# Storing half of the output earlier: the residual sum of the first 256 channels moved next to their inverse transform, and a new order for the whole program

## The chip, the cores and the metric

The kernel runs on one core of a Trainium2 chip. The metric is the device time of one execution in microseconds (us), lower being better. A core has one TensorE (PE, matmuls), VectorE (DVE), ScalarE (ACT), GpSimd (POOL, almost unused here) and SyncE (SP). In this kernel SP alone issues the transfers (DMAs) between DRAM and the on-chip memory (SBUF).

## What is computed

The input `u` has 2048 positions (tokens) of 512 channels. The result is the input plus a long convolution along the positions, scaled by a gate that an MLP computes:

```python
x = A_u
xn = _layernorm(x, axis=-1)
s = _A_ref(xn, A_A_re, A_A_im, A_B_re, A_B_im, A_C_re, A_C_im, A_log_dt, A_Dskip)
g = _silu(_B_ref(xn, B_w1, B_w2, B_w3, B_w4))
return x + s * g
```

`_A_ref` builds, for each channel, a kernel of 2048 taps from 128 complex exponentials, and convolves it with `xn` by a transform of length 4096 (`Kf = rfft(K)`, `Uf = rfft(u)`, `irfft(Uf * Kf)`), plus `u * Dskip`. `_B_ref` mixes tokens (`gelu(layernorm @ w1)`, a shift of each quarter of the channels by one or two positions, `@ w2`) and then runs an MLP of width 1376 (`gelu(layernorm(x1) @ w3) @ w4`), both with a residual.

## The kernel before

The tokens lie on the 128 partitions, 16 on each, so the result `X` is a tile of 128 x 16 x 512 float32. In DRAM the same data is addressed as `xv` (input) and `ov` (output) in four pieces of 32 partitions, `by_r` (L578), so every load of the input and every store of the result is four DMAs. `X` is worked on in eight groups `g` of two of the sixteen rows.

The stages are: loads; token mixing (layer norm, `w1`, `w2`); tables of exponentials for the convolution kernels (DVE and ACT); the first transform stage of the kernels (`kstage1`: results go to DRAM as `scr_Kfa` and `scr_Kfb`); the products of the spectra (`products`: loads `cst`, `uin`, `kin`, stores `scr_Zda`, `scr_Zdb`); the MLP (`w3` into the `pb` banks, gelu, `w4` into the `pa` banks); the gate, a silu on `X`; the inverse transform (`inverse(hf, g)`, L895: it loads a tile `zin` of 128 x 4 x 256, runs 16 small matmuls into a pair of `pc` or `pd` banks, and multiplies the pair into `X` on DVE); and `finish(g)`, L911. The convolution is done for two halves of the channels, `hf` 0 and 1, with 256 channels each (`DH`): letter a or b at the end of a scratch name is the half.

`finish(g)` loads the input again (the tiles `xr`, one for two groups, four DMAs of 32 x 2048), adds it to both halves of the group, 128 x 1024 elements in one DVE instruction, and stores the group with four DMAs of 32 x 1024, 128 KB each. It can only follow the inverse of both halves.

The order of the instructions is not written out by hand. Every step (`due`, L572) gives a due time to the instructions that follow it: a base from a few constants plus one entry of the table `SHIFT`. A list scheduler (`Plan.order`) places each instruction on its engine by the due times, dependences and modelled costs. It sets the order on PE, ACT, DVE and SP, and which of ACT and DVE makes some copies. Instructions of one engine then run in that order: one that waits holds all behind it, and that includes SP's DMAs. All instructions are issued from one line of a helper, L310 in the kernel before and L313 in the changed one, so the profile tells them apart by tiles.

Tiles that are reused are in rings: the loads of `zin` for the first half go round five buffers, those of the second half have eight.

Of the kernel before, what the change touches and what calls it, by code (L numbers as in the profile page):

```python
# [10 lines left out]
F32 = mybir.dt.float32  # L11
# [8 lines left out]
P = 128  # L20
L = 2048
D = 512
# [61 lines left out]
class Op:  # L84
# [10 lines left out]
SAME = {"PE": 0.0, "ACT": 0.13, "DVE": 0.1, "SP": 0.0}  # L95
TABLE_LOAD = 1.41
DMA_RATE = 300e3
LAND, PAD = 2.45, 0.16
BASE, FINE, END = 16512, 19840, 229368

KGC, QUAD = 3.25, 0.95
WARM = 40

SHIFT = (
# [21 lines left out]
)  # L126
Q0, QC = -778.0, 0.05
SWITCH = 2279.26
PREFERP, AVOIDP = 2674.41, 272.51
PREFER, AVOID = 3332.92, 790.65  # L130
PV, T0, TC = 257.0, 396.7, 309.52
LX, LC, LP, LW, LV = -4000.0, 0.11, -3964.6, -2693.7, -3696.7
M0, MC, WC = 807.9, 710.86, 0.25
H0, HC, SC = -3530.1, 638.4, 0.22
KA, PA, PAC, FA = -1045.1, -3015.7, 0.25, 592.1
KB, PB, PBC, FB = -157.1, -136.4, 0.08, 323.0
FC = 0.29


def mlp_due(g, jp):  # L140
# [3 lines left out]
class Plan:  # L144
# [105 lines left out]
    def order(self):  # L250
# [17 lines left out]
        while len(out) < len(ops):  # L268
# [4 lines left out]
            for o in pools[e]:  # L273
                if o.ready <= t + 0.02:
                    v = o.vt
                    if e == "ACT" and o.table and o.table != table:
                        v += SWITCH
                    if len(o.alts) > 1:
# [141 lines left out]
def kernel(  # L420
# [9 lines left out]
    V, A, T, Q = [Engine(plan, e) for e in ("DVE", "ACT", "PE", "SP")]  # L430
    E = Either(plan)

    xv = u[0].rearrange("(t r s) d -> r t s d", r=4, s=S)
    ov = out[0].rearrange("(t r s) d -> r t s d", r=4, s=S)
# [5 lines left out]
    DH = D // 2  # L440
# [7 lines left out]
    def area(nbytes):  # L448
        o = place[0]
        place[0] = o + nbytes  # L450
        assert place[0] <= END
        return o

    def at(offset, shape, dt, name):
        return nc.alloc_sbuf_tensor_at(name, shape, dt, offset=offset)[:]
# [37 lines left out]
    X = at(area(4 * S * D), [P, S, D], F32, "X")  # L493
    K2, K4 = 2048, 4096
# [8 lines left out]
    early = area(11 * K2)  # L503
# [25 lines left out]
    o = late + 8 * K4  # L529
# [10 lines left out]
        ),  # L540
    ]

    zinr = [Ring(early, K4, 5), Ring(o, K4, 8)]
    xrs = [late + 2 * K4 * k for k in range(3)] + [o + 10 * K4]
    assert o + 12 * K4 <= END

# [12 lines left out]
    def pp_pair():  # L559
        turn["pp"] += 1  # L560
        return bank[2 + turn["pp"] % 2]
# [9 lines left out]
    def due(t=None):  # L571
        plan.stage += 1  # L572
        t = plan.base = plan.base if t is None else t
        plan.vt = t + (SHIFT[plan.stage] if plan.stage < len(SHIFT) else 0)


    def by_r(sb, dr, to_dram=False):

        for r in range(4):
            a, d = sb[32 * r : 32 * r + 32], dr[r]  # L580
            Q.dma_start(d, a) if to_dram else Q.dma_start(a, d)
# [307 lines left out]
    def gate(g):  # L889
        due(FA + FC * g)  # L890
        X2 = X[:, 2 * g : 2 * g + 2]
        A.activation(X2, X2, AF.Silu)

    def inverse(hf, g):
        due((FA, FB)[hf] + FC * g)  # L895
        ch = slice(hf * DH, hf * DH + DH)
        zin = zinr[hf]([P, 4, DH], F32, "zin")
        Q.dma_start(zin, Zd[hf][:, 2 * g : 2 * g + 2, :, :, :].rearrange("r s e g d -> (s e g) r d"))
        py = [t[:, :DH] for t in pp_pair()]
        with plan.together(cost=0.55):  # L900
            for r in range(4):
                for a in range(2):
                    h = slice(64 * a, 64 * a + 64)
                    T.matmul(py[a][32 * r : 32 * r + 32], is2[h], zin[h, r], start=True, stop=True)
        for a in range(2):
            Xh = X[:, 2 * g + a, ch]
            V.tensor_mul(Xh, Xh, py[a])

    xr = []

    def finish(g):  # L911
        due(FB + FC * g)
        if g % 2 == 0:
            xr.append(at(xrs.pop(), [P, 4, D], F32, "xr"))
            by_r(xr[-1], xv[:, :, 2 * g : 2 * g + 4])
        X2 = X[:, 2 * g : 2 * g + 2]
        V.tensor_add(X2, X2, xr[-1][:, 2 * (g % 2) : 2 * (g % 2) + 2])
        by_r(X2, ov[:, :, 2 * g : 2 * g + 2], to_dram=True)


    def pow2_scale(cols, dst_s, dst_inv, target):
# [296 lines left out]
    for hf in range(2):  # L1218
        for g in range(8):
            inverse(hf, g)  # L1220
    for g in range(8):
        finish(g)
    with nc.allow_non_contiguous_dma(reason="parameters by state"), tc.manual_schedule():
# [26 lines left out]
```

## Time and profile before

| | us |
|---|---|
| median of 3 runs (lowest to highest) | 673.48 (673.35 to 673.55) |
| the profiled execution | 674.49 |
| its span in the profile | 672.7 |
| busy in the span: PE, weight loads (PEld) | 625.8 (93%), 414.4 |
| busy in the span: DVE, ACT | 540.7 (80%), 480.6 (71%) |

The page of the profile gives busy times of engines, and the chain of work that ended last, followed back from the last instruction. The table of windows gives the busy time of each engine in a stretch of the span, with the granted TensorE clock as a share of full speed and the share of the DMA engines in use. The timeline gives instructions in order of time. The sequencer of SP, which issues the DMAs, is called SPq; the duration of a DMA row is the time it held that sequencer, not the transfer. Times in the rows count from the start of the span.

### The profile page before, as it was taken

The page shows a single profiled execution, that of the slowest core. Times are in us where ns is not written, and L with a number is a line of the kernel's source. Part 1 is how long each engine was busy: PE and PEld are TensorE (multiplying, and loading weights), DVE is VectorE, ACT ScalarE, POOL GpSimd, SP SyncE. Part 2 cuts the span into 40 slices and gives each one's busy share as a digit, 9 for nine tenths or more (in the row PEclk, how much of TensorE's full clock was granted, in tenths as well). Part 3 has the DMA queues.
Part 4 walks back from the last instruction along what each step waited for, and adds up shares of the span by engine and source line. Part 5 has one row for each costly group of instructions (what it writes and reads, how often), then busy time and mean ns, then how long its engine had stood idle before and what let it go on. Part 6 is the DMA issues. An engine that isn't in the chain of part 4 may idle for free.

```text
span 672.7 us, 13855 instructions
## 1 busy us (share of the span) xinstructions
PE 625.8 (93%) x5526; PEld 414.4 (62%) x5526; DVE 540.7 (80%) x798; ACT 480.6 (71%) x1050; POOL 0.7 (0%) x6
## 2 busy tenths in 40 slices
PE   7489979899995999898999999999999999999984
PEld 7457858466464686665687576676675756556531
DVE  5898899999999999988999999998434154454557
ACT  3889899969938999987999999994246353223420
POOL 0000000000000000000000000000000000000000
PEclk9899999899998899998999999999999999999995
DMA  8955252422121111385343324328599568854997
GB/s 230 235 166 187 82 183 88 147 77 79 32 79 55 56 45 37 72 226 167 79 131 91 105 65 129 98 77 206 151 271 267 141 142 219 203 159 137 249 304 218
DMA packets 100751, 95.60 MB, mean 142 GB/s; under 512 B 48656, under 2 KB 81424, under 8 KB 99792
## 3 DMA queue, kind: packets, MB, share of 16 engines
q1 hardware_dynamic: 100688, 94.73, 50.3%
q8 instruction: 43, 0.70, 0.4%
q14 instruction: 20, 0.16, 0.1%
HBM read 61.16 MB, written 33.55 MB: 141 GB/s over the span
## 4 chain that ended last, share of the span: by engine, by line
PE 49%; DVE 37%; DMA 5%; ACT 4%; issue 4%; SPq 2%; DVEq 0%; ACTq 0%
PE pb L310 17%; PE pa L310 13%; DVE pt L310 11%; PE pc L310 10%; PE pd L310 9%; DVE kt L310 5%; DVE X L310 4%; DMA X<-in_A_u_dram 4%; DVE ghl L310 2%; DVE eg L310 2%; DVE pr L310 2%; DVE stats L310 2%; DVE pab L310 2%; SPq L310 2%; DVE w4h L310 1%
## 5 line engine op out<-in xcount | busy, mean ns | idle before, releaser
L310 PE MATMUL pb<-x1T,w3h 128*128 128x256 f16 (+1 forms) x1056 | 125.5, 274 | 1.2 <-DVE w3h L310 1.0
L310 PE MATMUL pa<-w4h,ghl 128*128 128x512 f16 (+1 forms) x528 | 124.5, 383 | 1.0 <-DVE w4h L310 0.8
L310 PEld LDWEIGHTS <-w3h 128*128 128x128 f16 (+1 forms) x1056 | 102.5, 101 | 30.0 <-issue 15.5
L310 ACT ACT_TABLE_LOAD x85 | 109.1, 1283 | 2.5 <-PEq L1238 0.7
L310 PEld LDWEIGHTS <-ghl 128*128 128x128 f16 (+1 forms) x528 | 49.3, 98 | 67.5 <-issue 16.5
L310 ACT ACTIVATE mag<-par 128x64 f32<-128x64 f32 x512 | 84.0, 277 | 6.5 <-DVE pt L310 6.3
L310 PE MATMUL pc<-kt 128*32 128x64 f32 x1024 | 84.1, 416 | 0.6 <-DVE kt L310 0.6
L310 PE MATMUL pc<-pt 128*32 128x64 f32 x1024 | 78.0, 388 | 0.0
L310 PE MATMUL pb<-xT,w 128*128 128x256 f32 x256 | 59.9, 390 | 2.8 <-ACT hT L310 2.8
L310 DVE SCALAR_TENSOR_TENSOR ghl<-g,wsc,ghl 128x512 f16<-128x512 f32 (+1 forms) x48 | 34.8, 733 | 31.0 <-ACT ghl L310 30.7
L310 PEld LDWEIGHTS pb<-xT,w 128*128 128x128 f32 x256 | 48.7, 194 | 15.7 <-issue 5.1
L310 PEld LDWEIGHTS pc<-pt 128*32 128x32 f32 x1024 | 56.2, 195 | 0.0
L310 PEld LDWEIGHTS pc<-kt 128*32 128x32 f32 x1024 | 48.4, 176 | 9.4 <-issue 5.9
L310 ACT ACTIVATE g<-pb,wsc 128x512 f32<-128x512 f32 (+1 forms) x48 | 32.8, 692 | 26.3 <-PE pb L310 25.9
L310 ACT ACTIVATE ghl<-g,wsc 128x512 f16<-128x512 f32 (+1 forms) x32 | 22.9, 722 | 27.1 <-PE pa L310 27.0
L310 DVE TENSOR_TENSOR kt<-mag,kt 128x1024 f32<-128x1024 f32 x32 | 40.8, 1275 | 0.0
L310 DVE SCALAR_TENSOR_TENSOR pt<-kt,pt 128x2080 f32<-128x2080 f32 x16 | 37.4, 2344 | 0.1
L310 ACT COPY z1e<-pd 128x256 f32<-128x256 f32 x36 | 12.7, 388 | 33.8 <-PE pd L310 33.8
L310 DVE TENSOR_TENSOR pr<-pc,kh 128x512 f32<-128x512 f32 x32 | 21.0, 686 | 19.4 <-PE pc L310 16.8
L310 PE MATMUL pd<-pr,cst 64*128 64x256 f32 x256 | 36.3, 402 | 0.0
L310 ACT ACTIVATE kt<-kt,halfpi 128x2080 f32<-128x2080 f32 x16 | 33.6, 2102 | 0.0
L310 DVE COPY z1e<-pd 128x256 f32<-128x256 f32 x28 | 11.6, 440 | 26.1 <-PE pd L310 26.1
(159 smaller groups left out, 981.2 us busy)
## 6 DMA issues: line engine op xcount, KB each, us to landing
wst<-in_B_w_dram SPq DMA_DIRECT2D x20, 512.0 KB, 3.8
scr_Ud<-ue SPq DMA_DIRECT2D x16, 512.0 KB, 3.3
scr_Kfa<-k1e SPq DMA_DIRECT2D x16, 256.0 KB, 3.5
uin<-scr_Ud SPq DMA_DIRECT2D x32, 128.0 KB, 3.0
cst<-c_gp SPq DMA_DIRECT2D x16, 256.0 KB, 2.6
kin<-scr_Kfa SPq DMA_DIRECT2D x32, 128.0 KB, 2.8
scr_Zda<-z1e SPq DMA_DIRECT2D x16, 256.0 KB, 2.2
xr<-in_A_u_dram SPq DMA_DIRECT2D x16, 256.0 KB, 6.4
```

Of the source, the lines that this page charges most:

```text
L310: ins = [getattr(self.engines[op.eng], name)(*args, **kw).ins for name, args, kw in op.calls]
```

## The change

A new step `finish_first(g)` follows the inverse of the first half of each group: it loads the 256 channels of the input (four DMAs of 32 x 2 x 256 into a tile `xh`, a ring of five buffers), adds them in one instruction of 128 x 2 x 256, and stores them (four DMAs of 32 x 2 x 256, 64 KB each). `finish` loads, adds and stores the second 256 channels alone. The 32 stores of 128 KB become 64 of 64 KB; the 16 loads of 256 KB (`xr`) become 16 of 128 KB and 32 of 64 KB (`xh`); the bytes stay the same. The 8 adds of 128 x 1024 become 16 of half the size. The ring of `zin` for the first half shrinks from five buffers to three, whose place the `xh` tiles take. The table `SHIFT` and the constants of the due times are all new.

```diff
-LAND, PAD = 2.45, 0.16
+LAND, PAD = 2.65, 0.16
...
 SHIFT = (
-    -2357, -12777, -7728, -8471, -1890, -5820, 626, 2299, 7826, 2606, 3103, -2484, -1642, 1374, 635, 1552,
...
+    17052, -33417, -23455, -9712, 1493, -1332, 7731, 14561, 22958, 13705, -431, -22670, -6774, 277, -9920, 4088,
...
-FC = 0.29
+FC = 0.08
...
-    zinr = [Ring(early, K4, 5), Ring(o, K4, 8)]
+    zinr = [Ring(early, K4, 3), Ring(o, K4, 8)]
+    xhr = Ring(early + 3 * K4, K2, 5)
...
+    def finish_first(g):
+        due(FA + FC * g)
+        x = xhr([P, 2, DH], F32, "xh")
+        by_r(x, xv[:, :, 2 * g : 2 * g + 2, :DH])
+        X2 = X[:, 2 * g : 2 * g + 2, :DH]
+        V.tensor_add(X2, X2, x)
+        by_r(X2, ov[:, :, 2 * g : 2 * g + 2, :DH], to_dram=True)
+
     xr = []
 
     def finish(g):
         due(FB + FC * g)
         if g % 2 == 0:
-            xr.append(at(xrs.pop(), [P, 4, D], F32, "xr"))
-            by_r(xr[-1], xv[:, :, 2 * g : 2 * g + 4])
-        X2 = X[:, 2 * g : 2 * g + 2]
+            xr.append(at(xrs.pop(), [P, 4, DH], F32, "xr"))
+            by_r(xr[-1], xv[:, :, 2 * g : 2 * g + 4, DH:])
+        X2 = X[:, 2 * g : 2 * g + 2, DH:]
         V.tensor_add(X2, X2, xr[-1][:, 2 * (g % 2) : 2 * (g % 2) + 2])
-        by_r(X2, ov[:, :, 2 * g : 2 * g + 2], to_dram=True)
+        by_r(X2, ov[:, :, 2 * g : 2 * g + 2, DH:], to_dram=True)
...
             inverse(hf, g)
+            if hf == 0:
+                finish_first(g)
```

The first place is the end of SP's queue (`zin<-scr_Zda` loads for an inverse of the first half, `zin<-scr_Zdb` of the second). Before, its last rows are:

```order
L310 DMA xr<-in_A_u_dram 32x2048 x8
L310 DMA scr_Zdb<-z1e 128x1024
L310 DMA zin<-scr_Zda 128x4x256
L310 DMA xr<-in_A_u_dram 32x2048 x2
L310 DMA zin<-scr_Zda 128x4x256 x2
L310 DMA zin<-scr_Zdb 128x4x256 x8
L310 DMA out_dram<-X 32x1024 x32
```

In the change, from the load of the tile `zin_645` on (an inverse of the first half; its buffer is the one that the tile `zin_639` had):

```order
L313 DMA zin<-scr_Zda 128x4x256
L313 DMA xr<-in_A_u_dram 32x4x256 x2
L313 DMA xh<-in_A_u_dram 32x2x256 x2
L313 DMA zin<-scr_Zdb 128x4x256
L313 DMA xh<-in_A_u_dram 32x2x256 x2
L313 DMA zin<-scr_Zdb 128x4x256 x6
L313 DMA zin<-scr_Zda 128x4x256 x2
L313 DMA zin<-scr_Zdb 128x4x256
L313 DMA out_dram<-X 32x2x256 x64
```

All stores still stand behind every load of `zin`, at the end of the queue. There are twice as many, and loads of `xh` are mixed with the loads ahead of them.

The second place is the end of DVE's queue, from the last instruction that takes an MLP result (`pa`) into `X`. Before:

```order
L310 SCALAR_TENSOR_TENSOR X_90<-pa1_94,wsc_79,X_90 128x512
L310 TENSOR_TENSOR X_90<-X_90,xr_652 128x1024
L310 TENSOR_TENSOR X_90<-X_90,pd0_99 128x256
L310 TENSOR_TENSOR X_90<-X_90,pd1_100 128x256
L310 TENSOR_TENSOR X_90<-X_90,xr_653 128x1024
L310 TENSOR_TENSOR X_90<-X_90,pc0_97 128x256
L310 TENSOR_TENSOR X_90<-X_90,pc1_98 128x256
```

In the change:

```order
L313 SCALAR_TENSOR_TENSOR X_90<-pa1_94,wsc_79,X_90 128x512
L313 TENSOR_TENSOR X_90<-X_90,xr_661 128x2x256
L313 TENSOR_TENSOR X_90<-X_90,pd0_99 128x256
L313 TENSOR_TENSOR X_90<-X_90,pd1_100 128x256
L313 TENSOR_TENSOR X_90<-X_90,xr_662 128x2x256
L313 TENSOR_TENSOR X_90<-X_90,pc0_97 128x256
L313 TENSOR_TENSOR X_90<-X_90,pc1_98 128x256
L313 TENSOR_TENSOR X_90<-X_90,xh_650 128x2x256
```

Behind the first of these rows DVE has 7 pairs of multiplications and 7 adds of 128 x 1024 before, and 6 pairs and 7 adds of 128 x 2 x 256 in the change. One of those seven adds is a first-half add (`xh_650`); the other seven first-half adds and two second-half adds stand ahead of this place. On PE, between the inverse of `zin_639` and the last MLP matmul there stand 96 matmuls into `pb`, 84 into `pa` and seven inverses.

## Rows read from the trace of the kernel before

**Rows 1.** The page: busy times, and the chain that ended last.

```profile
PE 625.8 (93%) x5526; PEld 414.4 (62%) x5526; DVE 540.7 (80%) x798; ACT 480.6 (71%) x1050; POOL 0.7 (0%) x6
...
PE 49%; DVE 37%; DMA 5%; ACT 4%; issue 4%; SPq 2%; DVEq 0%; ACTq 0%
```

**Rows 2.** Windows: length, then busy us (instructions) of PE, PEld, DVE, ACT, POOL; PEclk; DMA share; GB/s.

```profile
200.00:220.00 20.00, 11.82 (x145) 9.03 (x144) 19.97 (x28) 18.28 (x73) 0.00 (x0) 0.82 0.22 69
...
320.00:460.00 140.00, 139.69 (x1443) 97.60 (x1435) 138.82 (x169) 133.25 (x266) 0.00 (x0) 1.00 0.35 101
...
480.00:640.00 160.00, 159.43 (x1289) 97.51 (x1282) 72.69 (x140) 64.20 (x107) 0.00 (x0) 1.00 0.74 198
640.00:652.50 12.50, 12.50 (x105) 4.88 (x109) 5.22 (x9) 3.23 (x4) 0.00 (x0) 1.00 1.06 337
652.50:660.00 7.50, 4.38 (x64) 1.14 (x64) 6.89 (x13) 1.06 (x1) 0.00 (x0) 0.77 0.71 193
660.00:668.10 8.10, 4.29 (x48) 1.20 (x48) 7.96 (x13) 0.00 (x0) 0.00 (x0) 0.50 0.88 248
```

**Rows 3.** Timeline of DVE at the end: start us, us, engine, instruction, idle before.

```profile
653.85 0.74 DVE L310 SCALAR_TENSOR_TENSOR X<-pa,wsc,X 128x512 f32<-128x512 f32 x1
654.51 1.22 DVE L310 TENSOR_TENSOR X<-X,xr 128x1024 f32<-128x1024 f32 x1
...
664.11 0.75 DVE L310 TENSOR_TENSOR X<-X,pc 128x256 f32<-128x256 f32 x2
...
666.10 0.75 DVE L310 TENSOR_TENSOR X<-X,pc 128x256 f32<-128x256 f32 x2
666.88 1.23 DVE L310 TENSOR_TENSOR X<-X,xr 128x1024 f32<-128x1024 f32 x1
```

**Rows 4.** Timeline of PE around its last MLP matmuls and inverses.

```profile
622.50 2.79 PE L310 MATMUL pb<-x1T,w3h 128*128 128x256 f16 x24
...
649.73 2.77 PE L310 MATMUL pa<-w4h,ghl 128*128 128x512 f16 x12
652.43 0.66 PE L310 MATMUL pd<-zin,is 64*32 64x256 f32 x16
...
662.60 1.43 PE L310 MATMUL pc<-zin,is 64*32 64x256 f32 x16 [0.55 <-DVE X L310]
664.58 1.43 PE L310 MATMUL pc<-zin,is 64*32 64x256 f32 x16 [0.56 <-DVE X L310]
```

**Rows 5.** Timeline of SP's sequencer (SPq) at the end.

```profile
634.16 13.22 SPq L310 DMA_DIRECT2D zin<-scr_Zdb  x8
651.93 17.97 SPq L310 DMA_DIRECT2D out_dram<-X  x32
```

**Rows 6.** DMAs by tile: count, us held on SPq in ns (min/median/max), first and last start.

```profile
L310 SPq DMA_DIRECT2D out_dram<-X x32: 314/422/515, 651.9 to 669.5; - x32
...
L310 SPq DMA_DIRECT2D xr<-in_A_u_dram x16: 310/416/1273, 457.5 to 629.5; - x16
...
L310 SPq DMA_DIRECT2D uin<-scr_Ud x48: 573/597/1346, 306.0 to 592.7; - x48
...
L310 SPq DMA_DIRECT2D scr_Kfa<-k1e x16: 575/598/2462, 286.2 to 313.4; - x16
...
L310 SPq DMA_DIRECT2D Dt<-in_A_Dskip_dram x4: 558/568/743, 30.1 to 34.0; - x4
...
L310 SPq DMA_DIRECT2D wst<-in_B_w_dram x24: 333/380/420, 22.0 to 259.1; - x24
```

**Rows 7.** Timeline of SP: a pair of half-partition loads back to back.

```profile
571.80 1.24 SPq L310 DMA_DIRECT2D uin<-scr_Ud  x2
```

**Rows 8.** Groups by shape on DVE: count, busy us, mean ns of one.

```profile
L310 DVE TENSOR_TENSOR X<-X,xr 128x1024 f32<-128x1024 f32 x8 | 9.8, 1224 | 0.2
...
L310 DVE TENSOR_TENSOR X<-X,pd 128x256 f32<-128x256 f32 x16 | 6.0, 417 | 6.2 <-PE pd L310 6.1
...
L310 DVE TENSOR_TENSOR tm<-tm 128x512 f32<-128x512 f32 x3 | 2.1, 686 | 0.0
```

More of the change, by code (lines that the diff above doesn't have):

```diff
@@ L104 @@
 SHIFT = (
[21 rows of a table removed]
-)
[L127 to L136, printed above, removed]
-FC = 0.29
[24 rows of a table added]
+)
+Q0, QC = -3744.9, 0.33
+SWITCH = 12134.9
+PREFERP, AVOIDP = 8082.45, -17238.7
+PREFER, AVOID = 17860.0, 18183.0
+PV, T0, TC = 1856.7, 239.9, 2383.42
+LX, LC, LP, LW, LV = -4000.0, 0.08, -3071.8, 12710.4, 25366.6
+M0, MC, WC = 1389.9, 9549.57, 0.4
+H0, HC, SC = 4574.5, 2.54, 0.26
+KA, PA, PAC, FA = -2867.9, -39190.2, 0.07, 17550.1
+KB, PB, PBC, FB = 5280.7, 10111.3, 0.23, -6058.6
+FC = 0.08
 def mlp_due(g, jp):
```

43 rows, old and new, of the table SHIFT are left out of this document.

## The prediction

> **What bounds the kernel now.** I read the page first, then the windows, the timelines of the end, and last the DMAs by tile. The page [rows 1] says that PE is busy for 93% of the span and DVE for 80%, and that the chain that ended last runs over PE for 49% and over DVE for 37%. An average over such stages decides nothing, so the windows come next [rows 2]. From 320 to 460 us PE and DVE are both full (139.69 and 138.82 of 140 us), from 480 to 640 PE alone is (159.43 of 160): there only less PE work would help, and the change has as many matmuls as before. Time that is not PE's lies early (from 200 to 220 PE works 11.82 of 20 us) and at the end. The change names the end.
>
> I count the end from T, the end of the last MLP matmul: 649.73 + 2.77 = 652.50 [rows 4]. Three things run behind it. DVE takes the last MLP result into `X`, then multiplies and adds group after group until 666.88 + 1.23 = 668.11, or T + 15.6 [rows 3]. PE makes the last inverses. SP issues the 32 stores from 651.93 for 17.97 us, so to 669.90, or T + 17.4 [rows 5]. The span ends at 672.7, T + 20.2, that is 2.8 us behind the last issue: the last store's own transfer and what closes the program.
>
> **DVE's part at the end.** From the last instruction on `pa` (T + 1.35) to its end DVE takes 14.26 us now: 7 pairs of multiplications with a step of about 0.77 us (0.75 and a gap) and 7 adds of 1.22 [rows 3, 8]. The change leaves 6 pairs and 7 adds of 128 x 2 x 256. An add of 512 elements a partition, both operands in SBUF, takes 0.686 us [rows 8], about 0.65 as a step. That makes 0.66 + 6 x 0.77 + 7 x 0.65 = 9.8 us, so DVE alone would end at T + 11.2, 4.4 us earlier. Most of that lies beside something else. The last inverses go through one pair of `pc` banks; PE can start the next only when DVE has read the pair before. By then the granted clock is 0.50 [rows 2] (the lower level, 1.2 GHz; it stood at 1.00 until T, and fell as PE had 4.38 of 7.5 us of work, then 4.29 of 8.1), an inverse takes 1.43 us instead of the 0.66 it took at T [rows 4], and the pairs start 1.99 us apart (664.11 and 666.10) [rows 3]. The 1.22 us add lay hidden in that loop and hides there still when it is 0.65. In the change the first of five `pc` pairs can start about T + 4.1, the last four steps of 1.99 later at T + 12.1, and the last add ends about T + 13.5. Gain if only DVE and PE counted: 2.1 us.
>
> **SP's part at the end.** This decides. All 64 stores stand behind the last load of `zin`, so having the first half's sums early does not by itself start their stores early. When does that last load leave SP? `zin_645` needs the buffer of `zin_639`, since the ring has three. Between that inverse and T the order has 96 matmuls into `pb` (2.79 us for 24), 84 into `pa` (2.77 for 12) and seven inverses of 0.66 [rows 4]: 11.2 + 19.4 + 4.5 = 35, so `zin_645` is issued at T - 35. From it on there are ten loads of `zin`. Eight of them in a row take 13.22 us now [rows 5], 1.65 each, where SP waits for earlier loads to land: the DMA share is 1.06 in the window around them [rows 2]. Ten at this pace make 16.5 us, to T - 18.5. Of the six small loads between them each may cost 0.64 more, or nothing where SP waits for data anyway. So the stores start between T - 21 and T - 17; I take T - 19.
>
> Then 64 stores follow at a cost of s each on SP. No row shows a transfer of 32 partitions by two pieces of 256. The two nearest kinds give different answers [rows 6]. Stores and loads of 32 partitions in one piece each take 0.42 us (32 x 1024, 32 x 2048), with the gap to the next about 0.465. Transfers of part of the partitions in several pieces take 0.56 to 0.60: `uin`, 64 partitions in two or four pieces, 0.573 at least; `scr_Kfa`, 64 in two pieces, 0.575 at least; `Dt`, one partition in two pieces, 0.558. With the gap a pair of `uin` takes 1.24 us [rows 7], so 0.62 to 0.64 each. Full 128-partition loads in four pieces are cheap again (`wst`, 0.38). The new shape has few partitions and several pieces, in DRAM and in SBUF, and the three rows that share both never went under 0.55. I take s = 0.64 and keep 0.465 as the other end.
>
> With s = 0.64 the 64 stores take 41.0 us, from T - 19 to T + 22.0. The sums are ready in time: at T + 2.7, when the first of the last seven adds is done, SP still has some 30 stores to go. The end is then T + 22.0 + 2.8 = T + 24.8 against T + 20.2: **4.6 us later**.
>
> The page "Perfetto Trace Analysis" of the Trainium skill, section "What "DMA-bound" means", says that a kernel can be bound by the issuing sequencer, whose track is then solid with DMA slices, and that this is descriptor generation and no movement of data. The stores' row [rows 5] agrees in part: they follow each other almost solidly, though the adds bound them as well.
>
> **T itself.** Before T the change reorders much and adds little. Of the 8.2 us for which PE stands idle between 200 and 220 [rows 2], waiting for the first normalised tile of the MLP, I take off 0.9: by the order ACT and DVE have about that much less to do ahead of it. One more inverse (0.66) stands ahead of T. Together -0.2 us, with 2.5 either way for what such a reordering hides. The extra loads (16 `xr` and 32 `xh`, 23 us more of SP's time at 0.64) run while PE is the bound [rows 2] and are asked for long before they are used; I cost them at nothing.
>
> Sum: +4.6 - 0.2 = +4.4. The profiled execution took 674.49 us, 1.8 more than its span, and stands 1.0 above the median of 673.48. So 678.9 for an execution like the profiled one, and 677.9 for the median.
>
> **Rivals.**
> *Cheap stores (faster).* If a store of the new shape costs 0.465 like those of the same 32 partitions, 36 of the 64 are gone at T - 2.3; the other 28 start with the first of the last seven adds at T + 2.7 and end at T + 15.7, just behind DVE's T + 13.5. End T + 18.5: -1.7, with T -1.9, so 671.6. The point from which it decides: 64 s = 17.4 + 19 + 0.2 gives s = 0.572. For it: 32 partitions is what the stores have in common with the cheap rows. Against it: so few of its rows have several pieces. The same page of the skill, section "DMA Optimizations", says that splitting transfers may let some start sooner where the DMA engines are idle, which is this rival, and that small ones carry an overhead each, which is my forecast; by the first 671.6 would come out, by the second 677.9. The trace shows no idle DMA engines before T (share 1.06), but some behind it (0.71).
>
> *In between.* s from 0.55 to 0.594 puts the end within 1.35 us of now: about 673.5. The `Dt` row without a gap stands there. Also within it falls an s of 0.465 with a T that comes 1.5 us late.
>
> *Starved products (slower, another place).* In the stretch around 480 us SP must now issue some 18 loads of `xh` ahead of the stores of the last kernel spectra (`scr_Kfb`), which the second half's products wait for. At 0.64 that is 11.5 us of SP's time. If the stores are ready before SP is, PE stands still in the part where it is full now [rows 2]; I put the price at 3 to 6 us, 676.5 to 679.5, if the stores of the end are cheap.
>
> **How the numbers follow.** Chances: expensive stores 0.55, starved products 0.06, in between 0.14, cheap stores 0.25. The first two are slower. A difference under 0.2% (1.35 us) cannot be told from none. The forecast's own range is from s = 0.61 with a start at T - 21 (39.0 us, end T + 20.8, 0.4 us later with T's -0.2) to s = 0.65 with T - 17 (41.6, T + 27.4, 7.0 later), so 674 to 680.5; the unknown in T widens it to 682.5. The whole range reaches down to 671.0, below the cheap case.
>
> **What would show it.** Right: the stores on SPq are solid from before T, 0.6 us or more each, last beyond T + 20 and end after DVE by over 5 us. Wrong: a row of stores at 0.42 to 0.47, SP waiting for DVE between groups, and an end within 3 us of DVE's. In either case DVE should end about T + 13.5, with `pc` pairs 2 us apart at a granted clock of 0.50; pairs 1.3 us apart would say that the loop on the banks was not the cover. If PE shows idle time between 480 and 640, the starved products were right.

## The result, and the profile after the change

The change makes the kernel slower: a median of 678.09 us over 11 runs (675.68 to 680.34) against 673.55 us for the kernel before in the same comparison (673.35 to 676.6). The ratio is 1.0047, with a 95% interval of 1.0032 to 1.0063, so 3.2 us (2.2 to 4.2). The difference of the medians, 4.5 us, lies above that: six of the eleven runs of the kernel before stand at 673.35 to 673.55 and five at 674.54 to 676.6, and its median is the highest of the six. The profiled execution took 675.68 us, the lowest of the eleven, so its profile shows less of the loss than the median has; its span is 673.9 us against 672.7.

The busy shares of the page and the chain that ended last barely differ from [rows 1]:

```profile
PE 629.6 (93%) x5526; PEld 417.0 (62%) x5526; DVE 538.8 (80%) x798; ACT 477.3 (71%) x1051; POOL 0.7 (0%) x6
...
PE 45%; DVE 36%; ACT 5%; DMA 5%; issue 4%; SPq 3%; DVEq 0%; ACTq 0%
```

The end does. PE's timeline, with the last MLP matmul and two of the inverses behind it (answering to [rows 4]):

```profile
649.10 1.47 PE L313 MATMUL pa<-w4h,ghl 96*128 96x512 f16 x6
...
658.62 1.43 PE L313 MATMUL pc<-zin,is 64*32 64x256 f32 x16 [0.55 <-DVE X L313]
660.60 1.43 PE L313 MATMUL pc<-zin,is 64*32 64x256 f32 x16 [0.56 <-DVE X L313]
```

T is 649.10 + 1.47 = 650.57, which is 1.9 us earlier than before. DVE's last instructions (answering to [rows 3]):

```profile
660.13 0.75 DVE L313 TENSOR_TENSOR X<-X,pc 128x256 f32<-128x256 f32 x2 [0.51 <-PE pc L313]
660.91 0.69 DVE L313 TENSOR_TENSOR X<-X,xr 128x512 f32<-128x512 f32 x1
662.11 0.75 DVE L313 TENSOR_TENSOR X<-X,pc 128x256 f32<-128x256 f32 x2 [0.51 <-PE pc L313]
662.90 0.69 DVE L313 TENSOR_TENSOR X<-X,xr 128x512 f32<-128x512 f32 x1
```

DVE ends at 663.59, T + 13.0 (before T + 15.6), and now waits 0.51 us for PE in each of the last three steps of 1.98: nothing else covers the loop through the `pc` banks any more. SP's sequencer, from the last load of `zin` on (answering to [rows 5]), and the row of the stores by tile (answering to the first of [rows 6]), with the time from issue to landing below it:

```profile
633.91 1.40 SPq L313 DMA_DIRECT2D zin<-scr_Zdb  x1
635.40 36.09 SPq L313 DMA_DIRECT2D out_dram<-X  x64
```

```profile
L313 SPq DMA_DIRECT2D out_dram<-X x64: 315/431/1864, 635.4 to 671.1; - x64
...
DMA to landing us min/median/max: 1.7/1.7/5.5
```

From the eighth store on the row is:

```profile
643.00 28.50 SPq L313 DMA_DIRECT2D out_dram<-X  x57
```

The stores run from T - 15.2 to 671.49, T + 20.9, and the span ends at T + 23.3. For 7.9 us no engine but SP's sequencer has anything to do, which the windows show (columns as in [rows 2]):

```profile
635.40:643.20 7.80, 7.80 (x51) 3.37 (x49) 2.74 (x4) 2.99 (x6) 0.00 (x0) 1.00 0.97 310
643.20:650.57 7.37, 7.37 (x94) 2.85 (x87) 4.47 (x10) 1.49 (x2) 0.00 (x0) 1.00 0.43 110
650.57:663.60 13.03, 6.87 (x96) 1.94 (x96) 11.23 (x24) 1.06 (x1) 0.00 (x0) 0.71 0.53 136
663.60:671.50 7.90, 0.00 (x0) 0.00 (x0) 0.00 (x0) 0.00 (x0) 0.00 (x0) 0.50 0.52 135
```

From 643.20 on the DMA engines are only half in use (0.43 to 0.53), at 110 to 136 GB/s where the loads of `zin` got 310. It is not the transfers that fill SP's time but their issue: a store has landed 1.7 us after its issue, at the median as at the least, so the transfers do not pile up.

In short, the way from T to the end grew by 3.1 us (23.3 against 20.2) although DVE's part of it shrank by 2.6.

### The profile page after: what moved, and what is told of

Same layout as the page of the kernel before. It is cut to its first block, busy times and chain, and to the rows that moved or that the text cites. A ratio compares the mean times of both kernels' runs of the same rounds, so it can differ in the third digit from the quotient of the medians.

```text
span 673.9 us, 13919 instructions
## 1 busy us (share of the span) xinstructions
PE 629.6 (93%) x5526; PEld 417.0 (62%) x5526; DVE 538.8 (80%) x798; ACT 477.3 (71%) x1051; POOL 0.7 (0%) x6
## 4 chain that ended last, share of the span: by engine, by line
PE 45%; DVE 36%; ACT 5%; DMA 5%; issue 4%; SPq 3%; DVEq 0%; ACTq 0%
PE pb L313 18%; DVE pt L313 11%; PE pa L313 10%; PE pc L313 9%; PE pd L313 8%; DVE kt L313 6%; DVE X L313 3%; SPq L313 3%; DVE pr L313 3%; DMA X<-in_A_u_dram 2%; DVE stats L313 2%; DVE eg L313 2%; ACT mag L313 2%; DVE ghl L313 2%; DVE pab L313 2%
## 5 line engine op out<-in xcount | busy, mean ns | idle before, releaser
L313 PEld LDWEIGHTS <-w3h 128*128 128x128 f16 (+1 forms) x1056 | 102.6, 101 | 29.9 <-issue 15.2
L313 PE MATMUL pb<-xT,w 128*128 128x256 f32 x256 | 61.3, 396 | 1.7 <-ACT hT L313 1.7
L313 ACT ACTIVATE g<-pb,wsc 128x512 f32<-128x512 f32 (+1 forms) x48 | 32.4, 690 | 32.5 <-PE pb L313 32.1
L313 DVE SCALAR_TENSOR_TENSOR ghl<-g,wsc,ghl 128x512 f16<-128x512 f32 (+1 forms) x48 | 35.1, 739 | 24.4 <-ACT ghl L313 24.3
L313 DVE TENSOR_TENSOR kt<-mag,kt 128x1024 f32<-128x1024 f32 x32 | 42.8, 1336 | 0.3 <-ACT mag L313 0.3
L313 ACT ACTIVATE ghl<-g,wsc 128x512 f16<-128x512 f32 (+1 forms) x33 | 23.3, 710 | 24.6 <-PE pa L313 23.6
L313 DVE TENSOR_TENSOR pr<-pc,kh 128x512 f32<-128x512 f32 x32 | 21.0, 686 | 23.5 <-PE pc L313 17.1
L313 DVE SCALAR_TENSOR_TENSOR pt<-kt,pt 128x2080 f32<-128x2080 f32 x16 | 39.5, 2472 | 0.1
L313 ACT COPY z1e<-pd 128x256 f32<-128x256 f32 x45 | 15.3, 383 | 29.2 <-PE pd L313 28.9
L313 ACT ACTIVATE kt<-kt,halfpi 128x2080 f32<-128x2080 f32 x16 | 32.3, 2020 | 0.0
L313 ACT ACTIVATE pt<-pt 128x2080 f32<-128x2080 f32 x16 | 31.3, 1959 | 0.1
```

The lines of the kernel that those rows point to most:

```text
L313: ins = [getattr(self.engines[op.eng], name)(*args, **kw).ins for name, args, kw in op.calls]
```

## The experiments

Two theories stood against each other. Theory A: the row of stores on SP's sequencer is the loss. Theory B: the new due times are, ahead of T. In every trace the time is split at T. The first four kernels keep the changed kernel's due times.

**The changed kernel again** (`after_again`, no edit).

> The changed kernel once more, for a second trace of it. Theory A (the end of SP's queue is the loss): T, the end of the last MLP matmul, stays at 650 to 651 us, the 64 stores again leave SP in an almost solid row of 0.48 us each, and the end is T + 23. Theory B (the new due times are the loss, ahead of T): an execution near the median of 678 has a T of 653 or more, with the tail the same T + 23.

Measured: 679.65 us (677.19 to 681.32, 6 runs) against 674.58 for the kernel before on this chip, ratio 1.0079 (1.0057 to 1.0100). In its profiled execution, 677.19 us, T is 651.55 + 1.47 = 653.02 and the span 675.4, so the end is T + 22.4. The row of stores is there again:

```profile
637.38 35.65 SPq L313 DMA_DIRECT2D out_dram<-X  x64
```

So both moved: the tail is 2.2 to 3.1 us longer than before in both traces, and T itself varies by 2.4 us between two executions of one program.

**The ready stores moved ahead** (`hoist`). The 24 stores of the first half's groups 0 to 5 are taken out of SP's order and put behind the adds that they wait for:

```diff
-        for op in self.order():
+        for op in self.hoist(self.order()):
...
+            at = max(out.index(self.ops[d]) for d in op.deps)
...
+            out.insert(at + 1, op)
```

> The stores of the first half's groups 0 to 5 are moved on SP from behind the last load of zin to right behind their adds; all else keeps its place. Theory A: 20 to 24 stores of 0.48 us leave the end, DVE's adds bound it again, and the end comes at T + 17.5 to T + 18.5, 5 us before the changed kernel: 672.5 to 673.5. Theory B: the loss ahead of T stays, and the time is within 2 us of the changed kernel's 678.

Measured: 677.69 us (676.11 to 679.17, 7 runs), ratio 1.0050 (1.0032 to 1.0068). The time is what theory B had (within 2 us of 678) and not the 672.5 to 673.5 of theory A, but the tail is what theory A had: T is 657.48 and the span 675.9, so the end is T + 18.4. What the tail gave was lost ahead of T, at a wait that the move itself made. SP's and PE's timelines of this kernel:

```profile
620.13 3.01 SPq L324 DMA_DIRECT2D out_dram<-X  x4
623.18 0.43 SPq L324 DMA_DIRECT2D xh<-in_A_u_dram  x1
623.71 0.39 SPq L324 DMA_DIRECT2D zin<-scr_Zda  x1
```

```profile
628.47 0.98 PE L324 MATMUL pc<-zin,is 64*32 64x256 f32 x16 [2.57 <-DMA zin<-scr_Zda]
```

A load of `zin` stands behind four stores that hold SP for 3.01 us, and PE, which is the bound there, waits 2.57 us for it. Right behind the wait the granted clock is 0.62, where it was 1.00 before (columns as in [rows 2]):

```profile
628.47:633.00 4.53, 4.53 (x32) 2.00 (x33) 1.44 (x3) 0.00 (x0) 0.00 (x0) 0.62 0.91 265
```

Wait and clock together make 2.57 + 4.53 x 0.38 = 4.3 us, an estimate. From PE's first transpose of the MLP's input to T this kernel takes 442.4 us, `after_again` 438.1. A store next to its sum is free only where no load that PE waits for is queued behind it.

**Fewer stores at the same place** (`paired`). The stores of those six groups are made for two groups at once:

```diff
-        by_r(X2, ov[:, :, 2 * g : 2 * g + 2, :DH], to_dram=True)
+        if g > 5:
+            by_r(X2, ov[:, :, 2 * g : 2 * g + 2, :DH], to_dram=True)
+        elif g % 2:
+            by_r(X[:, 2 * g - 2 : 2 * g + 2, :DH], ov[:, :, 2 * g - 2 : 2 * g + 2, :DH], to_dram=True)
```

> The first half's stores of groups 0 to 5 are made for two groups at once, 12 stores of 128 KB for 24 of 64 KB, at the same place of SP's queue. Theory A: the cost is by the store and not by the byte, so SP is 12 x 0.48 = 5.8 us sooner and the end comes at T + 18.5 to T + 19.5, 4 to 5 us before the changed kernel. If the stores cost by the byte (bandwidth), the time stays at 678. Theory B: within 2 us of 678.

Measured: 674.98 us (672.23 to 676.66, 12 runs), ratio 1.0002 (0.9987 to 1.0016): 4.7 us below the changed kernel in the same comparison, with the same bytes. T is 654.73 and the span 673.4, so the end is T + 18.7. The cost is by the store and not by the byte, as theory A had it. But T is later than in both traces of the changed kernel, though every engine has the changed kernel's order up to the stores; the account of `after_32` comes back to this.

**The due times without the split** (`late_full`). `finish_first` is empty, and `finish` is that of the kernel before:

```diff
     def finish_first(g):
         due(FA + FC * g)
-        x = xhr([P, 2, DH], F32, "xh")
...
-            xr.append(at(xrs.pop(), [P, 4, DH], F32, "xr"))
+            xr.append(at(xrs.pop(), [P, 4, D], F32, "xr"))
```

> The due times of the change without its split: adds of 128 x 1024 and 32 stores of 128 KB at the end as before, no loads xh. Theory A: the end is that of the kernel before, T + 20, and T is that of the changed kernel (650.6 in its profile, against 652.5), so 671 to 672.5, faster than before. Theory B: the new order costs time ahead of T, and the median is above 675 as the changed kernel's is.

Measured: 677.86 us (676.68 to 679.5, 6 runs), ratio 1.0049 (1.0031 to 1.0067). A miss for theory A taken alone, and the number that theory B had (above 675). T is 654.31 and the span 676.4, so the end is T + 22.1: these due times leave DVE more work behind T (its last add ends at 671.79, T + 17.5), and T came 1.8 us later than in [rows 4]. The experiment changes the end's order too, so it says that the due times are no gain here, but not how much of that lies ahead of T.

**The split alone, with 64, 48 and 32 stores.** The next three have the due times of the kernel before, and its order on PE but for inverses near the end that stand six MLP matmuls later (three in `split_64`, one in the other two). Only the adds are split, and the first half's part is moved next to its inverse. They use the `xr` tiles as before, so there are no loads of `xh`. All stores stand behind the last load of `zin`.

```diff
-        X2 = X[:, 2 * g : 2 * g + 2]
-        V.tensor_add(X2, X2, xr[-1][:, 2 * (g % 2) : 2 * (g % 2) + 2])
-        by_r(X2, ov[:, :, 2 * g : 2 * g + 2], to_dram=True)
+        x = xr[-1][:, 2 * (g % 2) : 2 * (g % 2) + 2]
+        second = plan.vt
+        for ch, vt in ((slice(0, DH), first[g]), (slice(DH, D), second)):
+            plan.vt = vt
+            X2 = X[:, 2 * g : 2 * g + 2, ch]
+            V.tensor_add(X2, X2, x[:, :, ch])
...
+            by_r(X2, ov[:, :, 2 * g : 2 * g + 2, ch], to_dram=True)
```

`split_48` stores the first half for two groups at once, and `split_32` the second half too, with the edit shown for `paired`.

> The split alone, on the kernel before with its due times and its xr loads: first-half adds and second-half adds apart, 64 stores of 32 x 2 x 256, all behind the last load of zin, as in the change. The order of PE and of all other transfers is that of the kernel before. Theory A (SP's row of stores is the loss): SP starts them at T - 5 and needs 64 x 0.48 = 30.7 us, so the end is T + 28.5 against T + 20.2 before: 8 us slower, 682. Theory B (the due times are the loss): the same time as before, or 2 us less by the shorter adds at the end.

> As split_64, with the first half's stores made for two groups at once: 48 stores for 64. Theory A: 48 x 0.48 = 23 us from T - 5, end at T + 20.9, within 1 us of the kernel before. Theory B: no different from split_64.

> As split_48, with the second half's stores for two groups at once too: 32 stores of 128 KB, as many as before. Theory A: SP is no longer the bound; the loop on the pc banks is, the last add ends at T + 13.5 to T + 14, and the end is T + 18.2 to T + 19: 1.2 to 2 us faster than before. Theory B: no different from split_64.

Measured, against 674.90 us for the kernel before (29 runs): 686.31, 678.85 and 673.42 us; ratios 1.0162 (1.0136 to 1.0187), 1.0058 (1.0040 to 1.0077) and 0.9976 (0.9958 to 0.9994). The rows of stores of the three, one trace each:

```profile
647.22 34.40 SPq L317 DMA_DIRECT2D out_dram<-X  x64
```

```profile
647.50 27.16 SPq L317 DMA_DIRECT2D out_dram<-X  x48
```

```profile
648.61 20.49 SPq L317 DMA_DIRECT2D out_dram<-X  x32
```

T is 652.2, 652.6 and 653.4, and the spans are 684.0, 677.0 and 672.0, so the ends are T + 31.8, T + 24.4 and T + 18.6. `split_48` and `split_32` have one order on PE and DVE; in `split_64` two inverses stand six MLP matmuls later ahead of T, and one instruction of DVE (on `ghl`) earlier. 16 stores more cost 7.2 us of SP's time from 48 to 64, 0.45 each. DVE's last add ends at T + 13.5 in `split_64` (665.06 + 0.69) and at T + 13.5 in `split_32` (666.22 + 0.69): it does not feel the stores. The first two ends are some 3.4 us later than expected. The reason is that the row starts slowly, while the loads of `zin` are still under way. The waits of SP in `split_64` from 640 us on show it (us in total, times, longest):

```profile
SPq L317 <- DMA zin<-scr_Zdb: 3.0, 3, 1.1
```

and the longest store of its row was held for 1.36 us. The expectation had counted 0.48 from the first store on.

Theory B fails here: with the due times of the kernel before the loss is larger (1.6% for `split_64`), not gone. In the changed kernel, whose due times and loads are new as well, the row starts at T - 15 and not at T - 5, and it is some 6 to 8 us faster than `split_64` by the ratios: with 64 stores the new order is a gain over the old one.

**The banks of the last inverses alternated** (`split_32_alt`, and once more as `split_32_alt_2`).

```diff
-        py = [t[:, :DH] for t in pp_pair()]
+        pair = pp_pair() if hf == 0 else bank[3 - g // 2 % 2]
+        py = [t[:, :DH] for t in pair]
```

> As split_32, with the pairs of banks of the second half's inverses dealt out in the order in which they run, so that they alternate between pc and pd. If the loop of one bank pair at the lower clock (1.99 us a group) bounds split_32, the pairs come 1.4 us apart here, the last add ends at T + 11.5 to T + 12 and the end is T + 16.5 to T + 17: 3 to 4 us faster than before, about 671. If DVE or SP bound split_32, no more than 0.5 us is won on it.

> split_32_alt once more, beside the next one on the same chip: 0.3 to 0.6% faster than before, end at T + 17.3.

Measured: 672.24 us against 674.90, ratio 0.9954 (0.9936 to 0.9973), and 671.30 us against 674.85, ratio 0.9944 (0.9927 to 0.9961). The ends are T + 17.3 and T + 17.8. The win over `split_32` is about 1 us, with intervals that overlap, and not the two expected: the last three inverses still go through the `pc` pair, and DVE's last add comes at T + 12.6 in both traces. This is the fastest version of the study that was timed twice, 0.5% below the kernel before.

**Half of the stores issued by ACT** (`split_64_act`, `split_32_alt_act`). ACT is idle at the end; two of every four stores are moved to its sequencer, and nothing else:

```diff
+        act = {i for n, i in enumerate(act) if n % 4 > 1}
+        for i in act:
+            self.ops[i].eng = "ACT"
```

> split_64 with the two last of every four stores issued by ACT, which is idle then, in place of SP: the same 64 transfers of 64 KB, 32 on each sequencer. If the sequencer's 0.48 us a store is the bound, the row halves and the end is DVE's again: T + 17 to T + 18.5, 13 us before split_64, near 672. If the transfers themselves are (rate of the DMA engines, or a cost by 1 KB piece), the end stays near split_64's T + 31.8.

> split_32_alt with two of every four stores issued by ACT. If its last four stores in a row on SP (4 x 0.48) bound its end, two rows of two take 0.96 us off: T + 16.3 against T + 17.3. If the last store's own time is what is left, no difference.

Measured: `split_64_act` 673.77 us, ratio 0.9982 (0.9962 to 1.0002), 12.5 us below `split_64` (timed in another comparison) with the same 64 transfers. Its two rows, and a window of them (columns as in [rows 2]):

```profile
646.00 20.14 SPq L322 DMA_DIRECT2D out_dram<-X  x32
```

```profile
653.29 15.68 ACTq L322 DMA_DIRECT2D out_dram<-X  x32
```

```profile
653.30:666.10 12.80, 5.84 (x82) 1.72 (x80) 10.03 (x22) 1.04 (x1) 0.00 (x0) 0.75 0.91 251
```

T is 651.1 and the span 671.4, so the end is T + 20.3, later than expected, because ACT's row starts only behind ACT's last silu (653.29) and then needs 15.68 us, 0.49 a store. The DMA engines, 0.91 in use, took the stores at 251 GB/s, where `split_64` had 136 with 0.53 (655 to 680 us): the sequencer was the bound. ACT brings its own queue too, but in `split_64` a store landed 1.7 us after its issue, at the median as at the least, so SP's queue was not what was full. `split_32_alt_act` gave 671.40 us, ratio 0.9949 (0.9930 to 0.9968), end T + 16.9: no difference from `split_32_alt_2` in time, though the end comes 0.4 and 0.9 us sooner than in the two traces of `split_32_alt`. With 32 stores a second sequencer gains nothing that these runs can tell.

**The changed kernel with 32 stores** (`after_32`). All stores for two groups at once, the changed kernel's due times, and its order on PE, DVE and ACT.

> The changed kernel with its own due times, all stores made for two groups at once: 32 stores of 128 KB, at the end of SP's queue as in the change; PE, DVE and ACT have the changed kernel's order. The tail is then T + 17.5 to T + 18.5. Theory A alone (the stores are all of the loss): 672.5 to 673.5, 0.3% faster than before. With a loss of the new due times ahead of T (2 us between the MLP's first transpose and T in the traces so far): 674 to 676, no faster than before.

Measured: 674.67 us (671.05 to 675.67, 12 runs), ratio 0.9988 (0.9971 to 1.0005). The profiled execution is the lowest, 671.05: T is 651.1 and the end T + 18.2. So the tail is 2.0 us shorter than before, and the median is only 0.2 below it: some 1 to 2 us are lost ahead of T. One part of that is in the traces. From PE's first transpose of the MLP's input to T:

```profile
212.29 1.96 PE L313 MATMUL pd<-ident,x1n 128*128 128x128 f32 x8 [4.59 <-ACT x1n L313]
```

is 650.57 - 212.29 = 438.3 us in the changed kernel, 438.1 in `after_again` and in `after_32`; in the kernel before it is 436.1 (its transposes start at 216.40), in `split_64` 436.0 and in `split_32` 436.5. So that stretch costs 2 us more with the new due times. One more inverse stands in it (0.66 us), and between 340 and 480 us PE is idle for 2.2 us, where it was for 0.3 before; between 480 and 640 it is idle for 0.6 us less (160.00 of 160 us busy against 159.43). The window before, then in the changed kernel, and the waits of PE in it (the kernel before has none there):

```profile
340.00:480.00 140.00, 139.69 (x1468) 96.83 (x1466) 129.90 (x166) 120.60 (x244) 0.00 (x0) 1.00 0.40 113
```

```profile
340.00:480.00 140.00, 137.80 (x1444) 96.75 (x1438) 127.82 (x166) 116.81 (x245) 0.00 (x0) 1.00 0.42 122
```

```profile
PE pd L313 <- DVE pr L313: 1.1, 2, 0.7
PE pb L313 <- ACT g L313: 0.9, 1, 0.9
```

On the other side the transposes come sooner, at 212.3, 214.9 and 213.0 us against 216.4, 216.2 and 216.9. In these executions of the changed order, the lowest of their comparisons, T comes 1.9 us earlier than before, 0.5 later and 1.4 earlier. In an execution near the median nothing makes up for the 2 us: that of `paired` took 675.20 us (median 674.98), its transposes start at 216.06, and T is 653.26 + 1.47 = 654.73, 2.2 us later than before.

```profile
216.06 1.97 PE L313 MATMUL pd<-ident,x1n 128*128 128x128 f32 x8 [4.66 <-ACT x1n L313]
...
653.26 1.47 PE L313 MATMUL pa<-w4h,ghl 96*128 96x512 f16 x6
```

## Why the prediction came out right

The time was forecast at 677.9 us (+4.4), and 678.09 was measured (+4.5 between the medians; +3.2 by the ratio, +2.2 to +4.2 with its interval). The mechanism at the end is shown: all stores stand behind the last load of `zin`, SP's sequencer is solid with them, and it ends 7.9 us behind DVE. Taking stores away (`paired`, 64 to 48 to 32) or giving them a second sequencer (`split_64_act`) takes the loss away, with the same bytes.

That the sum came within 0.2 us is luck: its terms were not right, and their errors cancelled. Of the signs set down beforehand, the row was solid from before T, lasted beyond T + 20 and ended over 5 us behind DVE, as forecast; but a store at 0.42 to 0.47 was the sign of being wrong, and that is where it lies. The bound was seen rightly, the reason given for its being slow was not.

- *The price of a store.* I took s = 0.64, from `uin`, `scr_Kfa` and `Dt`, which share few partitions and several pieces. The row says 0.431 at the median; with the gap of some 0.045 that is 0.475, just as for the stores in one piece (0.422). So 64 x 0.475 = 30.4 us in place of 41.0. Two pieces of 1 KB a partition cost SP hardly more than one of 4 KB, and the changed kernel's loads of 32 partitions in two and in four such pieces took 0.426 and 0.424 (`xh`, `xr`). What makes the three dear rows dear stays open; few partitions with several pieces, on which I had put it, are not enough.
- *The start.* I had T - 19; the trace says T - 15.2, 3.8 us later. `zin_645` left SP at 618.26, T - 32.3 and not T - 35: the inverse of `zin_639` ended at T - 33.4, and loads of `xh` held SP until T - 32.4. From there to the first store SP took 17.1 us and not 16: with `zin_645` itself eleven loads of `zin` leave SP, where I had counted ten.
- *The beginning of the row.* I had it at full pace from the first store. It took 36.09 us in place of 30.4. Of the 5.7 us lost, 4.3 went with the first seven stores, while the loads of `zin` were still landing: they took 7.6 us (635.40 to 643.00), the other 57 took 28.50.
- Together: -10.6 + 3.8 + 5.7 = -1.1, so SP ends at T + 20.9 and not T + 22.0. What follows the last issue took 2.4 us and not 2.8. The tail cost 3.1 us (2.2 in the second trace) where 4.6 had been forecast.
- *DVE's part.* T + 13.5 forecast, T + 13.0 measured. The last four of the five `pc` pairs stood 1.98 us apart at a granted clock of 0.50, the first step was 1.53: as forecast, the shorter adds lay hidden in the loop on the banks. With that loop loosened (`split_32_alt`) another 1 us was there.
- *T.* I had -0.2, with 2.5 either way. The idle time of PE in 200 to 220 fell, as argued and by more (from 8.2 to 6.0 us), and one more inverse was counted. The 1.9 us more of idle PE between 340 and 480 were not. In the two traces T is 650.6 and 653.0, but both executions were the lowest of their comparisons; in that of `paired`, near its median and with the same order up to the stores, T is 2.2 us later than before. So of the median's loss some 2 to 3 us lie in the tail and some 2 ahead of T, where I had 4.6 and -0.2. Why the transposes of one order start anywhere from 212.3 to 216.1 us stays open.

The rival *cheap stores* had the right price and yet the wrong sign, since it rested on the same start and the same full pace. Its point of decision, 0.572 a store, moves to 0.42 when 9.5 us of start and slow beginning are put in (36.6 - 9.5 = 27.1 for 64). The price alone did not decide: with the measured price and the rest as I had it, I would have forecast a gain. The rival *starved products* did not happen: PE had 160.00 of 160 us of work between 480 and 640.

Of the Trainium skill, the page "Perfetto Trace Analysis", section "DMA Optimizations", says that where descriptor generation is the bottleneck it may help to balance DMAs across the engines that can issue them: `split_64_act` agrees, with 12.5 us. The page "DMA: Bandwidth & Descriptors", section "Issuing engines are not separate DMA queues", says that this saves only the sequencer's time, usually small next to the transfer. Here it was not small: 0.475 us of issue for each 64 KB, with the DMA engines 0.53 in use.

## What to carry to other kernels

Count the DMAs that stand behind the last load, times the cost of one issue on its sequencer (here 0.475 us for 64 KB and 0.465 for 128 KB), and set that beside what bounds the end. Sums made earlier did not help while their stores held the end, and a store put early must not stand ahead of a load that the busy engine waits for. Here, with the due times of the kernel before, the split became a gain of 0.2% once the stores were made as few as before, and of 0.5% with the banks alternated.

## What was not expected of the hardware

The first small stores behind the large loads left the sequencer slowly: in the changed kernel 12 of them took 9.83 us, where 12 in mid-row take 12 x 0.475 = 5.7.

```profile
635.40 9.83 SPq L313 DMA_DIRECT2D out_dram<-X  x12
```

Part of that, 3.1 us, is waiting for the loads to land (SP's waits from 633 us on):

```profile
SPq L313 <- DMA zin<-scr_Zda: 2.1, 2, 1.1
SPq L313 <- DVE ghl L313: 1.7, 2, 1.5
...
SPq L313 <- DMA zin<-scr_Zdb: 1.0, 1, 1.0
```

SP's DMAs share eight semaphores in turn, so each waits until the DMA eight places before it has landed, and the sixth to eighth store stood behind such loads. The first store was itself held for 1.86 us. The view names a result of DVE there, `ghl`, which is no sum; what held the store is not shown.

And the time of one program varied by 4.7 us between its lowest and highest run (675.68 to 680.34), 2.4 us of T between two traces, with the granted clock between 20 and 40 us at 0.88 in the one and 0.76 in the other. With a dozen runs of a kernel the interval of its ratio still reached 1.0 to 1.4 us to either side.
